# Gated mix of two 32-head attentions: one order of steps for a head, and one PSUM tile of seven banks

## The chip, the cores and the metric

The kernel runs on one core of one Trainium2 chip. The metric is the device time of one execution in microseconds (us): 2744.99 us, the median of three runs that lie between 2744.64 and 2745.0 us. The profile is of one more execution of the same program; its own span is 2743.5 us.

## The reference, cut to what matters

```python
def ref(x, wqkv, wo):                      # B=1, S=2048, D=512, H=32 heads of 16
    qkv = (x @ wqkv).reshape(B, S, 3, H, Dh).transpose(2, 0, 3, 1, 4)
    q, k, v = qkv[0], qkv[1], qkv[2]
    scores = einsum("bhqd,bhkd->bhqk", q, k) * (Dh ** -0.5)
    p = softmax(scores, axis=-1)
    o = einsum("bhqk,bhkd->bhqd", p, v)
    return o.transpose(0, 2, 1, 3).reshape(B, S, D) @ wo

g = sigmoid((x * gate_w).sum(-1, keepdims=True))
return g * ref(x, A_wqkv, A_wo) + (1 - g) * ref(x, B_wqkv, B_wo)
```

Two attentions over the same 2048 tokens give 64 heads in all, each with a 2048 x 2048 matrix of scores.

## The kernel before

**Prologue.** Queries, keys and values of both sides are projected by TensorE (`qk_tile`, `project_v`), each result as twelve accumulating matmuls into one PSUM bank of 128 x 512. ScalarE rounds a query or key tile (line 310), VectorE takes the rest of it (line 311), and both go to HBM; ScalarE copies a value tile out (line 346). There are 64 tiles of queries and keys and 32 of values. Between the value tiles, six at a time, the first 96 chunks of maxima are made.

**A head** is 16 rounds of 128 keys. Three kinds of work run over it, for three different heads or rounds at once:

- *Maxima, for a head two ahead.* The softmax needs each query's largest score. A chunk is one matmul of 128 queries by 512 keys (`scores_bank`, line 148) and a VectorE reduction of it (`max_plain`, line 153). In every second row block two chunks are made as a difference: ScalarE takes a Relu of one (`max_rise`, line 160), and VectorE adds it to the other while it reduces (`max_pair`, line 165). A head has 48 plain chunks, 8 rises and 8 pairs.
- *Scores and exponentials, for the present head.* A matmul of 128 keys by 512 queries (`score`, line 210), whose contraction also subtracts the maximum, and the exponential of it by ScalarE into the tile `p` (line 212); four of these fill a round, 64 a head.
- *Products with the values, two rounds behind* (`attend`, line 689). They accumulate in a PSUM bank of their own, `acc`. A quarter of a round is four small matmuls side by side; several quarters run as a burst. At a head's end ScalarE copies `acc` out (line 710).

Matmuls of the first two kinds contract over 48 or 50 rows, in the upper or the lower half of the array by turns (`rows`), so that two of them run side by side.

**What sets the order.** There is no scheduler: `tc.manual_schedule()` keeps the order in which the program is written, engine by engine, and the framework adds the waits on semaphores. The order comes from strings, four rounds at a time: `e` is a score with its exponential, `m` a plain maximum, `D` a rise, `A` a pair, and a digit a burst of so many quarters. `FULL` is used inside a head, `EDGE` where a head begins and ends, `LATE` once no maxima are left (the last 22 rounds). A head has 20 bursts: 16 of three quarters and 4 of four.

**PSUM.** Its eight banks are `acc`, three tiles of a pool `ps_m` and four of a pool `ps_st`. Each tile is one bank, handed out in rotation: maxima take from `ps_m`, scores and rises from `ps_st`. A matmul into a tile waits for the reader of that slot's tile before.

```python
    ps_m = ctx.enter_context(tc.tile_pool(name="ps_m", bufs=3, space=PSUM))
    ps_st = ctx.enter_context(tc.tile_pool(name="ps_st", bufs=4, space=PSUM))
    ps_acc = ctx.enter_context(tc.tile_pool(name="ps_acc", bufs=1, space=PSUM))
    acc = ps_acc.tile([P, 512], F32, name="acc")
```

The output projections (`project_out`, `project_part`, line 558) come in between, at bursts, when a side's heads are done, and once more at the end; each takes a bank from `result_bank`. Their 52 tiles are 16 of twelve matmuls, 15 of nine and 21 of three.

Of the kernel before, what the change touches and what calls it, by code (L numbers as in the profile page):

```python
# [32 lines left out]
P = 128  # L33
# [11 lines left out]
LEAD = 6  # L45
SCALE = DH ** -0.5
HALVES = (0, 64)
SC = 3 * DH


@with_exitstack
def gated_mha(ctx: ExitStack, tc: tile.TileContext, xT, x, wqkv_a, wo_a, wqkv_b, wo_b, gate_w, out):
# [29 lines left out]
    warm = ps_m.tile([P, 512], F32, name="ps_m")  # L82
    for i in range(14):
        pe.matmul(warm, ident, ident.unsqueeze(1).to_broadcast([P, 4, P]), start=True, stop=True)  # L84
    q_st, k_st, x_st = [], [], []
# [40 lines left out]
    mxp, rises = {}, {}  # L126
    turn = [0]

    def rows():
        turn[0] ^= 1  # L130
        return HALVES[1 - turn[0]]
# [6 lines left out]
    def scores_bank(m, c, early=False):  # L138
        h, t = divmod(m, NT)
        st = c == "rise" or early and c % 2  # L140
        ps = (ps_st if st else ps_m).tile([P, 512], F32, name="ps_st" if st else "ps_m")
        b = rows()
        q = q_st[h % 3]
        if c == "rise":
            k = x_st[h % 2][b:b + SC]
        else:
            k = k_st[h % 3][b:b + SC, c * 512:(c + 1) * 512]
        pe.matmul(ps, q[b:b + SC, t * P:(t + 1) * P], k, start=True, stop=True)  # L148
        return ps, mxp[h][:, t]
# [40 lines left out]
    ring = []  # L190

    def result_bank():
        if ring:
            ring[0] = (ring[0] + 1) % 7
        if not ring or ring[0] % 2:
            return ps_m.tile([P, 512], F32, name="ps_m")
        return ps_st.tile([P, 512], F32, name="ps_st")

    def score(r, c):
# [4 lines left out]
        kk, cc = (4 * (kt % 4) + c, kt // 4) if h == NH - 1 else (kt, c)  # L204
        b = rows()
        if r < 2 and c % 2:
            ps = ps_m.tile([P, 512], F32, name="ps_m")
        else:
            ps = result_bank() if ring else ps_st.tile([P, 512], F32, name="ps_st")
        pe.matmul(ps, k[b:b + SC + 2, kk * P:(kk + 1) * P], q[b:b + SC + 2, cc * 512:(cc + 1) * 512],  # L210
                  start=True, stop=True)
        act.activation(pt[r][:, c * 512:(c + 1) * 512], ps, AF.Exp, scale=SCALE)  # L212


    vpool = ctx.enter_context(tc.tile_pool(name="vpool", bufs=2))
# [10 lines left out]
    with tc.tile_pool(name="xs", bufs=1) as xs, tc.tile_pool(name="pro", bufs=2) as pro:  # L226
# [57 lines left out]
        def qk_tile(i, cc):  # L284
            s, g, isk = blocks[i]
            w = wblocks[s, isk * DM + g * P]
            ps = ps_st.tile([P, 512], F32, name="ps_st")
            steps = [(k, p) for p in PARTS for k in range(KC)]
            for n, (k, (a, b)) in enumerate(steps):
                pe.matmul(ps, w[a][:, k], (xh, xl)[b][cc][:, k], start=n == 0, stop=n == 3 * KC - 1)  # L290
            return ps

        def first_tiles():
            banks = [ps_st.tile([P, 512], F32, name="ps_st") for i in range(2)]
# [41 lines left out]
        def project_v(s, t):  # L336
            hi, lo = wblocks[s, 2 * DM]
            c, o = divmod(t * P, 512)
            ps = ps_st.tile([P, 512], F32, name="ps_st")
            n = 0  # L340
            for a, b in ((xh[c], hi), (xl[c], hi), (xh[c], lo)):
                for k in range(KC):
                    pe.matmul(ps, a[:, k, o:o + P], b[:, k], start=n == 0, stop=n == 3 * KC - 1)  # L343
                    n += 1
            v = ps.rearrange("p (h d) -> p h d", h=H)
            act.copy(v_st[t % 2][:, :, 0:16], v)  # L346
            nc.sync.dma_start(vd[s][t * P:(t + 1) * P, :], v_st[t % 2].rearrange("p h d -> p (h d)"))
# [373 lines left out]
            done[0] += qb - qa  # L721
            n -= qb - qa

    FULL = "mme3emmeem4meeemAe", "3emmeeem3meeemA3DeD"
    EDGE = "eemm4mDmemDe3emeemAe", "3emmeeem3emem3eAe"
    LATE = "ee4eeee4ee"
    projects, row_ops = [], []

    def due(first):
        for r in (first, first + 1):  # L730
            for fn, a in later.pop(r, ()):
                if fn is project_out:
                    projects.append(a)
                else:
                    fn(*a)
# [4 lines left out]
    to_rise = iter(range(first + 4, ROUNDS, 2))  # L740

    load_stacks(2)
    r = 2
    while r < ROUNDS:
        m = r + NT + LEAD
        if m >= ROUNDS and not ring:
            ring.append(6)
            turn[0] = 0
        order = (EDGE if r % NT == 2 and r > 2 else FULL)[0] + (EDGE if r % NT == 14 else FULL)[1]
        if m >= ROUNDS:  # L750
            order = LATE
        n = order.count("e") // 4
        due(r)
        if r % NT == 2 and r // NT + 2 < NH:
            if r // NT:
                load_stacks(r // NT + 2)
            new_maxima(r // NT + 2)
        scored = bursts = 0
        for step in order:
            if step == "e":  # L760
                if scored == 8:
                    due(r + 2)
                score(r + scored // 4, scored % 4)
                scored += 1
            elif step == "m":
                max_plain(*next(plain))
            elif step == "D":
                for k in to_rise:
                    max_rise(k)
                    break  # L770
            elif step == "A":
                max_pair(next(pairs))
            else:
# [11 lines left out]
        if m < ROUNDS and (m + 4) % NT == 0:  # L785
            row_ops += [(max_split, m // NT), (max_rows, m // NT)]
        r += n
    attend_next(4)
    for fn, a in mid.pop((ROUNDS - 2, 2)):
        fn(*a)  # L790
# [28 lines left out]
```

## Time and profile before

| | |
|---|---|
| median of three runs | 2744.99 us (2744.64 to 2745.0) |
| span of the profiled execution | 2743.5 us |
| instructions | 64283 |
| PE (TensorE matmul) busy | 2733.8 us, 100% |
| DVE (VectorE) busy | 2411.5 us, 88% |
| ACT (ScalarE) busy | 2410.8 us, 88% |
| POOL (GpSimd) busy | 262.2 us, 10% |
| DMA, mean | 84 GB/s |
| first products with the values | 289.1 us |

A busy PE is not a PE at its peak: matmuls overlap, and the end that the trace gives one is modelled. So the intervals between the starts of instructions are read here, not the shares. PEld is the load of a matmul's weights; it carries the wait for the bank, and the matmul follows it at once.

### The profile page before, as it was taken

To read this page: it belongs to the slowest core of one execution; us is meant where nothing else is said; L and a number is where in the kernel's file an instruction comes from. 1 tells how busy PE (TensorE), PEld (TensorE's weight loads), DVE (VectorE), ACT (ScalarE), POOL (GpSimd) and SP (SyncE) were. 2 spreads that over 40 slices of the span, in tenths; PEclk is the share of its full clock that TensorE was granted. 3 is DMA by queue.
4 is the path that set the end of the run, shared out by engine and by line. 5 is a ranking of instruction groups with operands and counts; after the bars stand their busy time and mean duration, and the time that the engine had idled before them with its cause. 6 is when DMAs were issued, how large, how long until landed. Compare 5 with 4: busy or idle time off the path is not lost.

```text
span 2743.5 us, 64283 instructions
## 1 busy us (share of the span) xinstructions
PE 2733.8 (100%) x25446; PEld 1418.7 (52%) x25446; DVE 2411.5 (88%) x4473; ACT 2410.8 (88%) x4794; POOL 262.2 (10%) x467
## 2 busy tenths in 40 slices
PE   9999999999999999999999999999999999999998
PEld 7787544444444444444444555544444444445543
DVE  5444899999999999999999978899999999998895
ACT  4222899999999999999999978899999999998787
POOL 2010112110000000000100232000000001002202
PEclk9999999999999999999999999999999999999999
DMA  8583434333333233333423534223333333344312
GB/s 286 181 262 153 93 74 81 62 70 62 74 67 60 52 60 67 62 64 62 85 52 54 123 78 92 48 49 62 78 62 63 59 66 65 62 87 83 80 36 95
DMA packets 95603, 231.25 MB, mean 84 GB/s; under 512 B 26182, under 2 KB 35878, under 8 KB 82758
## 3 DMA queue, kind: packets, MB, share of 16 engines
q1 hardware_dynamic: 91590, 216.65, 36.1%
q0 software_dynamic: 2560, 8.91, 1.1%
q8 instruction: 201, 3.29, 0.6%
q10 hardware_dynamic: 1152, 1.57, 0.2%
q14 instruction: 100, 0.82, 0.1%
HBM read 158.13 MB, written 68.94 MB: 83 GB/s over the span
## 4 chain that ended last, share of the span: by engine, by line
PE 99%; DVE 1%; DMA 0%; issue 0%; SPq 0%; DVEq 0%; POOL 0%; POOLq 0%
PE acc L689 38%; PE ps_st L210 24%; PE ps_m L148 19%; PE ps_st L290 6%; PE ps_st L148 5%; PE ps_st L343 3%; PE ps_m L558 3%; PE ps_st L558 0%; PE ps_m L84 0%; PE ps_st L299 0%; DVE o_acc L575 0%; DMA o_num<-od 0%; DVE mxp L153 0%; PE ps_m L210 0%; DVE rise L165 0%; DMA od<-ev 0%
## 5 line engine op out<-in xcount | busy, mean ns | idle before, releaser
L212 ACT ACTIVATE p<-ps_st 128x512 f32<-128x512 f32 x4050 | 2076.8, 629 | 95.3 <-PE ps_m L148 56.1
L153 DVE TENSOR_REDUCE mxp<-ps_m 128x1 f32<-128x512 f32 x3048 | 1934.8, 684 | 125.2 <-PE ps_st L148 46.0
L210 PE MATMUL ps_st<-q_st,k_st 50*128 50x512 f32 x4054 | 1269.5, 433 | 0.0
L148 PE MATMUL ps_m<-k_st,q_st 48*128 48x512 f32 x3548 | 1223.8, 439 | 0.3
L689 PE MATMUL acc<-p,vg 128*17 128x128 f32 (+3 forms) x15664 | 1129.8, 392 | 0.5 <-DVE ev L703 0.4
L210 PEld LDWEIGHTS ps_st<-q_st,k_st 50*128 50x128 f32 x4054 | 614.0, 184 | 436.4 <-ACT p L212 382.7
L148 PEld LDWEIGHTS ps_m<-k_st,q_st 48*128 48x128 f32 x3548 | 604.2, 184 | 268.7 <-DVE mxp L153 222.1
L689 PEld LDWEIGHTS acc<-p,vg 128*17 128x17 f32 x15664 | 323.1, 96 | 404.2 <-issue 330.7
L165 DVE CUSTOM_DVE_ANT_0 rise<-ps_m,rise 128x512 f32<-128x512 f32 x500 | 341.2, 682 | 16.6 <-PE ps_m L148 13.1
L160 ACT ACTIVATE rise<-ps_st 128x512 f32<-128x512 f32 x500 | 300.1, 601 | 16.6 <-PE ps_st L210 0.8
L148 PE MATMUL ps_st<-x_st,q_st 48*128 48x512 f32 x500 | 195.4, 451 | 0.0
L175 POOL CAST mparts<-mrow 128x16 fp32r<-128x16 f32 x64 | 12.7, 198 | 1875.9 <-DVE mrow L174 1875.9
L148 PEld LDWEIGHTS ps_st<-x_st,q_st 48*128 48x128 f32 x500 | 78.0, 184 | 119.5 <-ACT p L212 119.2
L310 ACT CAST part<-ps_st 128x512 fp32r<-128x512 f32 x64 | 37.0, 589 | 111.6 <-PE ps_st L290 95.6
L311 DVE TENSOR_TENSOR part<-ps_st,part 128x512 fp32r<-128x512 f32 x64 | 43.7, 690 | 93.7 <-ACT part L310 70.2
L346 ACT COPY v_st<-ps_st 128x512 f32<-128x512 f32 x32 | 18.8, 588 | 84.2 <-PE ps_st L343 82.5
L558 PE MATMUL ps_m<-wo,ot 128*128 128x512 f32 x348 | 83.0, 393 | 1.0
L558 PEld LDWEIGHTS ps_m<-wo,ot 128*128 128x128 f32 x348 | 64.4, 188 | 19.6 <-issue 4.6
L290 PE MATMUL ps_st<-xh,whi 128*128 128x512 f32 x224 | 59.9, 389 | 0.0
L290 PE MATMUL ps_st<-xh,wlo 128*128 128x512 f32 x224 | 59.9, 389 | 0.0
L290 PE MATMUL ps_st<-xl,whi 128*128 128x512 f32 x224 | 59.9, 389 | 0.0
L545 POOL TENSOR_TENSOR o_num<-o_num,rb 128x512 f32<-128x512 f32 x28 | 35.9, 1287 | 221.7 <-DMA rb<-rd 221.7
(120 smaller groups left out, 946.4 us busy)
## 6 DMA issues: line engine op xcount, KB each, us to landing
k_st<-kd SPq DMA_DIRECT2D x128, 256.0 KB
q_st<-qd SPq DMA_DIRECT2D x128, 256.0 KB
qd<-part SPq DMA_DIRECT2D x32, 512.0 KB
kd<-part SPq DMA_DIRECT2D x32, 512.0 KB
k_st<-kd SPq DMA_DIRECT2D x128, 128.0 KB
q_st<-qd SPq DMA_DIRECT2D x128, 128.0 KB
od<-ev SPq DMA_DIRECT2D x63, 256.0 KB
vd<-v_st SPq DMA_DIRECT2D x32, 272.0 KB
```

The source lines that it names most:

```text
L148: pe.matmul(ps, q[b:b + SC, t * P:(t + 1) * P], k, start=True, stop=True)
L153: dve.tensor_reduce(o[:, c:c + 1], ps, op=ALU.max, axis=AX.X)
L160: act.activation(rises[m], ps, AF.Relu)
L165: dve.tensor_tensor_reduce(out=rise, in0=ps, in1=rise, scale=1.0, scalar=LOWEST, op0=ALU.add, op1=ALU.max, accum_out=o[:, 0:1])
L210: pe.matmul(ps, k[b:b + SC + 2, kk * P:(kk + 1) * P], q[b:b + SC + 2, cc * 512:(cc + 1) * 512], start=True, stop=True)
L212: act.activation(pt[r][:, c * 512:(c + 1) * 512], ps, AF.Exp, scale=SCALE)
L290: pe.matmul(ps, w[a][:, k], (xh, xl)[b][cc][:, k], start=n == 0, stop=n == 3 * KC - 1)
L310: act.copy(pt[0][:, sl], ps)
L311: dve.tensor_tensor(pt[1][:, sl], ps, pt[0][:, sl].bitcast(F32), op=ALU.subtract)
L343: pe.matmul(ps, a[:, k, o:o + P], b[:, k], start=n == 0, stop=n == 3 * KC - 1)
L558: pe.matmul(ps, ot[a][:, slot, tt * P:(tt + 1) * P], wt[b][:, g], start=first and i == 0, stop=last and i == 2)
L689: pe.matmul(acc[32 * c:32 * c + 17, qa * P:qb * P], v[:, 4 * a + c if final else kt, j], p[:, c * 512 + qa * P:c * 512 + qb * P], start=fi ...
```

## The change

The three PSUM pools become one pool with two tiles: `acc`, and `ring`, one tile of seven banks of which every result takes a slice. `take` keeps the banks in the order of their last use and gives the oldest, or the one of a given rank. Up to the tenth round of the first head the prologue and the first rounds stay with three banks for the one use and four for the other. From there on, 62 times, a head's 16 rounds follow one string, `HEAD`, with the ranks of its banks in `RANKS`; a run of `q` is a burst of so many quarters, and `W` is two score matmuls into two banks and one exponential of 1024 over both. A head has 38 single exponentials and 13 wide ones, 48 plain maxima, 8 rises and 8 pairs as before, and 21 bursts (1 of one quarter, 2 of two, 13 of three, 5 of four). `r` marks the two small steps that close a head's maxima. `LATE` stays.

```diff
-    ps_m = ctx.enter_context(tc.tile_pool(name="ps_m", bufs=3, space=PSUM))
-    ps_st = ctx.enter_context(tc.tile_pool(name="ps_st", bufs=4, space=PSUM))
-    ps_acc = ctx.enter_context(tc.tile_pool(name="ps_acc", bufs=1, space=PSUM))
-    acc = ps_acc.tile([P, 512], F32, name="acc")
+    psum = ctx.enter_context(tc.tile_pool(name="psum", bufs=1, space=PSUM))
+    psb = psum.tile([P, NB, 512], F32, name="ring")
+    acc = psum.tile([P, 512], F32, name="acc")
+    age = list(range(NB))
+
+    def take(rank=0, among=range(NB)):
+        b = [b for b in age if b in among][rank]
+        age.remove(b)
+        age.append(b)
+        return b
+
+    def m_bank():
+        return psb[:, take(0, range(3))]
+
+    def st_bank():
+        return psb[:, take(0, range(3, NB))]
...
+    def chosen():
+        return psb[:, take(ranks.pop(0))] if ranks else None
...
-        ps = (ps_st if st else ps_m).tile([P, 512], F32, name="ps_st" if st else "ps_m")
+        ps = chosen() or (st_bank if st else m_bank)()
...
+        if n == 2:
+            b0, b1 = take(ranks.pop(0)), take(ranks.pop(0))
+            if b1 < b0:
+                chunks.reverse()
+            wide = [psb[:, b0], psb[:, b1]]
+            ps = psb[:, min(b0, b1):max(b0, b1) + 1:abs(b1 - b0)]
...
+        for i, c in enumerate(chunks):
+            kk, cc = (4 * (kt % 4) + c, kt // 4) if h == NH - 1 else (kt, c)
+            b = rows()
+            pe.matmul(wide[i] if n == 2 else ps, k[b:b + SC + 2, kk * P:(kk + 1) * P],
+                      q[b:b + SC + 2, cc * 512:(cc + 1) * 512], start=True, stop=True)
+        c = min(chunks)
+        p = pt[r][:, c * 512:(c + n) * 512]
+        act.activation(p.rearrange("p (n x) -> p n x", n=2) if n == 2 else p, ps, AF.Exp, scale=SCALE)
...
-    FULL = "mme3emmeem4meeemAe", "3emmeeem3meeemA3DeD"
-    EDGE = "eemm4mDmemDe3emeemAe", "3emmeeem3emem3eAe"
+    FULL = "mmeqqqemmeemqqqqmeeemAe", "qqqemmeeemqqqmeeemAqqqDeD"
+    HEAD = ('mqqqemmeemeqqmDemqmemreDqqqmeAmWqqqWAmeerqqqmDememqqqqemmWemqqqemWmmeqqqmeWDmqqq'
...
+    for h in range(1, NH - 1):
+        ranks.extend(int(x) for x in RANKS)
+        run(HEAD, h)
+        assert not ranks
```

What stands on TensorE in the middle of a head before, with the semaphores that a row waits for (Activation is ScalarE's count, DVE VectorE's; L210 is a score, L148 a maximum, L689 a product with the values):

```order
L689 MATMUL acc<-p,vg 17x256 x4
L210 MATMUL ps_st<-q_st_160,k_st_161 128x512 [waits Activation_49]
L148 MATMUL ps_m<-k_st_2348,q_st_2347 128x512 [waits DVE_49] x2
L210 MATMUL ps_st<-q_st_160,k_st_161 128x512 [waits Activation_49] x3
L148 MATMUL ps_m<-k_st_2348,q_st_2347 128x512 [waits DVE_49]
L689 MATMUL acc<-p,vg 17x256 x4
L689 MATMUL acc<-p,vg 17x128 x4
L148 MATMUL ps_m<-k_st_2348,q_st_2347 128x512 [waits DVE_49]
L210 MATMUL ps_st<-q_st_160,k_st_161 128x512 [waits Activation_49] x3
L148 MATMUL ps_m<-k_st_2348,q_st_2347 128x512 [waits DVE_49] x2
```

A score waits for ScalarE and a maximum for VectorE, whatever stands ahead of it. And the same place in the changed program (L233 is a score, L167 a maximum, L714 a product):

```order
L167 MATMUL ring<-k_st_160,q_st_159 128x512 [waits Activation_49]
L233 MATMUL ring<-q_st_2139,k_st_2140 128x512 [waits DVE_49]
L167 MATMUL ring<-k_st_160,q_st_159 128x512 [waits Activation_49]
L167 MATMUL ring<-k_st_160,q_st_159 128x512 [waits DVE_49]
L233 MATMUL ring<-q_st_2139,k_st_2140 128x512 [waits DVE_49]
L233 MATMUL ring<-q_st_2139,k_st_2140 128x512
L714 MATMUL acc<-p,vg 17x384 x4
L233 MATMUL ring<-q_st_2139,k_st_2140 128x512 [waits Activation_49]
L233 MATMUL ring<-q_st_2139,k_st_2140 128x512
L167 MATMUL ring<-k_st_160,q_st_159 128x512 [waits Activation_49]
L167 MATMUL ring<-k_st_160,q_st_159 128x512 [waits DVE_49]
L233 MATMUL ring<-q_st_2139,k_st_2140 128x512 [waits DVE_49]
```

Here the engine that a matmul waits for is the one that reads the result of the `ring` matmul ahead of it: ScalarE behind a score, VectorE behind a maximum; only the second matmul of a `W` (the rows without a wait) has none. The counts in the built program say the same. At one place a score goes to bank 0, and its exponential brings ScalarE's count to 1931; the next matmul, a maximum into bank 4, waits for 1931. Its reduction brings VectorE's count to 1969; the next, a maximum into bank 5, waits for 1969. Before, a score waited for the exponential four scores back.

The prologue, where six maxima (L148, now L167) stand between two value tiles (L343, now L368), before:

```order
L343 MATMUL ps_st<-wvlo,xh_180 128x512 x4
L148 MATMUL ps_m<-k_st_161,q_st_160 128x512
L148 MATMUL ps_st<-k_st_161,q_st_160 128x512 [waits DVE_49]
L148 MATMUL ps_m<-k_st_161,q_st_160 128x512
L148 MATMUL ps_st<-k_st_161,q_st_160 128x512 [waits DVE_49]
L148 MATMUL ps_m<-k_st_161,q_st_160 128x512
```

and now:

```order
L368 MATMUL ring<-wvlo,xh_174 128x512 x4
L167 MATMUL ring<-k_st_155,q_st_154 128x512 [waits Activation_49]
L167 MATMUL ring<-k_st_155,q_st_154 128x512 [waits DVE_49] x5
L368 MATMUL ring<-wvhi,xh_174 128x512 [waits DVE_49]
L368 MATMUL ring<-wvhi,xh_174 128x512 x3
```

Each of the six now waits, the first for the copy of the value tile ahead of it, the others for the maximum ahead of them, and the next value tile for the last of the six.

More of the change, by code (lines that the diff above doesn't have):

```diff
@@ L48 @@
 SC = 3 * DH
+NB = 7
 @with_exitstack
@@ L192, in result_bank, with score @@
     def result_bank():
[L193 to L199, printed above, removed]
+        return psb[:, take()] if ring else m_bank()
+    def score(r, c, n=1):
         h, kt = divmod(r, NT)
@@ L293, in first_tiles @@
         def first_tiles():
-            banks = [ps_st.tile([P, 512], F32, name="ps_st") for i in range(2)]
+            banks = [st_bank() for i in range(2)]
             for k in range(KC):
@@ L338, in project_v @@
             c, o = divmod(t * P, 512)
-            ps = ps_st.tile([P, 512], F32, name="ps_st")
+            ps = st_bank()
             n = 0
@@ L742, in gated_mha, with next_chunk, products, run @@
     load_stacks(2)
[L743 to L764, printed above, removed]
+    at_chunk = [2 * NQ]
+    def next_chunk(n=1):
+        r, c = divmod(at_chunk[0], NQ)
+        at_chunk[0] += n
+        if c == 0 and r % 2 == 0:
+            due(r)
+            if r % NT == 2 and r // NT + 2 < NH:
+                if r // NT:
+                    load_stacks(r // NT + 2)
+                new_maxima(r // NT + 2)
+        return r, c
+    def products(n):
+        for a in projects:
+            project_out(*a)
+        projects.clear()
+        turn[0] = 0
+        attend_next(n)
+        if row_ops:
+            fn, *a = row_ops.pop(0)
+            fn(*a)
+    def run(order, h=None):
+        steps = [fn for fn in (max_split, max_rows)]
+        i = 0
+        while i < len(order):
+            step = order[i]
+            n = 1
+            if step == "q":
+                n = len(order[i:]) - len(order[i:].lstrip("q"))
+                products(n)
+            elif step == "r":
+                steps.pop(0)(h)
+            elif step in "eW":
+                w = 2 if step == "W" else 1
+                score(*next_chunk(w), w)
             elif step == "m":
@@ L772, in gated_mha @@
                 max_pair(next(pairs))
+            i += n
+    cycle = FULL[0] + FULL[1]
+    run(cycle)
+    run(cycle[:-3] + "DeD".replace("D", "", 2))
+    for h in range(1, NH - 1):
+        ranks.extend(int(x) for x in RANKS)
+        run(HEAD, h)
+        assert not ranks
+    row_ops += [(max_split, NH - 1), (max_rows, NH - 1)]
+    r = at_chunk[0] // NQ
+    assert r + NT + LEAD == ROUNDS and done[0] == 4 * (r - 2)
+    ring.append(6)
+    turn[0] = 0
+    while r < ROUNDS:
+        due(r)
+        scored = bursts = 0
+        for step in LATE:
+            if step == "e":
+                if scored == 8:
+                    due(r + 2)
+                score(r + scored // 4, scored % 4)
+                scored += 1
             else:
```

25 lines of the change are left out of this document (12 added, 13 removed).

## The prediction

> **What bounds the kernel now.** I read the page first, then the waits, then the stretch of heads without output projections, then single instructions.
>
> ```profile
> span 2743.5 us, 64283 instructions
> PE 2733.8 (100%) x25446; PEld 1418.7 (52%) x25446; DVE 2411.5 (88%) x4473; ACT 2410.8 (88%) x4794; POOL 262.2 (10%) x467
> L212 ACT ACTIVATE p<-ps_st 128x512 f32<-128x512 f32 x4050 | 2076.8, 629 | 95.3 <-PE ps_m L148 56.1
> L153 DVE TENSOR_REDUCE mxp<-ps_m 128x1 f32<-128x512 f32 x3048 | 1934.8, 684 | 125.2 <-PE ps_st L148 46.0
> ```
>
> Three engines are nearly full. The per-head copy of `acc` is a clock: its starts in a quiet stretch give the time of a head.
>
> ```profile
> L710 ACT COPY ev<-acc x8: 587/592/594, 1028.6 to 1287.8; 128x512 f32<-128x512 f32 x8
> 1114.16 7.67 ACT L212 ACTIVATE p<-ps_st 128x512 f32<-128x512 f32 x15
> PEld ps_st L210 <- ACT p L212: 382.7, 879, 0.9
> PEld ps_m L148 <- DVE mxp L153: 222.1, 488, 0.9
> ```
>
> Seven heads in 259.2 us are 37.03 us each. ScalarE has 73 instructions in a head (64 exponentials, 8 rises, the copy), and fifteen in a row start (7.67 - 0.60) / 14 = 0.505 us apart: 73 of them are 36.9 us. So a head goes at ScalarE's pace, with VectorE and TensorE close behind, and this works only because the engines overlap: several banks are full at a time, and while ScalarE and VectorE each empty one, TensorE fills the next. TensorE's waits for a reader, the last two rows, are short ones (0.9 us at the longest).
>
> **What the change does to that.** By its words it lets all results share seven banks and spares 13 starts of an exponential. But the order above shows another thing: in the changed program each matmul into `ring` waits for the reader of the one ahead of it, whatever bank that used, because the seven banks are now one tile. Then matmul, reader, matmul, reader form one chain, with one bank in use, and the seven are worth nothing. The price of the chain is a round trip, and its four parts have rows:
>
> ```profile
> 1112.17 0.50 PE L148 MATMUL ps_st<-x_st,q_st 48*128 48x512 f32 x1
> 1112.71 0.60 ACT L160 ACTIVATE rise<-ps_st 128x512 f32<-128x512 f32 x1
> ...
> 1076.67 0.60 ACT L160 ACTIVATE rise<-ps_st 128x512 f32<-128x512 f32 x1
> 1077.32 0.18 PEld L210 LDWEIGHTS ps_st<-q_st,k_st 50*128 50x128 f32 x1 [0.19 <-ACT rise L160]
> ...
> 256.36 0.50 PE L148 MATMUL ps_m<-k_st,q_st 48*128 48x512 f32 x1
> 256.89 0.69 DVE L153 TENSOR_REDUCE mxp<-ps_m 128x1 f32<-128x512 f32 x1 [2.64 <-PE ps_st L148]
> ...
> 1104.37 0.68 DVE L153 TENSOR_REDUCE mxp<-ps_m 128x1 f32<-128x512 f32 x1
> 1105.10 0.18 PEld L148 LDWEIGHTS ps_m<-k_st,q_st 48*128 48x128 f32 x1 [0.22 <-DVE mxp L153]
> ```
>
> A matmul into an idle array takes 0.50; ScalarE starts 0.54 after its start, works 0.60, and 0.05 after its end (1077.27 to 1077.32) the released load begins. *A ScalarE step is 0.54 + 0.60 + 0.05 = 1.19 us.* VectorE starts 0.53 after, works 0.69, and 0.05 later (1105.05 to 1105.10) comes the load: *a VectorE step is 1.27 us.* A pair's instruction is of the same size as a reduction (682 against 684 ns in the page), so it counts as one.
>
> *A wide step.* No exponential of 1024 is in the trace. Its two matmuls have no wait between them and go side by side; the length of the reader I take from a ScalarE cast that comes in both widths.
>
> ```profile
> L277 ACT CAST xh<-raw 128x512 fp32r<-128x512 f32 x8 | 4.9, 618 | 1.2 <-DMA raw<-in_xT 1.0
> L277 ACT CAST xh<-vg 128x1024 fp32r<-128x1024 f32 x4 | 4.1, 1054 | 0.0
> ...
> 1108.46 0.50 PE L210 MATMUL ps_st<-q_st,k_st 50*128 50x512 f32 x1
> 1108.46 0.49 PE L148 MATMUL ps_m<-k_st,q_st 48*128 48x512 f32 x1
> ```
>
> 512 more elements cost 1.054 - 0.618 = 0.44, so 0.54 + 0.60 + 0.44 + 0.05 = 1.63. Bounds: 1.2 if the width were free, 2.4 if it were two steps; the cast is the nearest row, and the bounds move a head by 13 x 0.4 to 0.8 us.
>
> *The bursts* do not touch `ring`, so they run while the reader of the last matmul works.
>
> ```profile
> 1103.28 0.39 PE L148 MATMUL ps_m<-k_st,q_st 48*128 48x512 f32 x1
> 1103.60 1.05 PE L689 MATMUL acc<-p,vg 128*17 128x512 f32 x8
> 1104.58 0.18 PEld L148 LDWEIGHTS ps_m<-k_st,q_st 48*128 48x128 f32 x1 [0.85 <-DVE mxp L153]
> ...
> 1111.40 0.84 PE L689 MATMUL acc<-p,vg 128*17 128x384 f32 x8
> 1112.17 0.18 PEld L148 LDWEIGHTS ps_st<-x_st,q_st 48*128 48x128 f32 x1 [0.64 <-ACT p L212]
> ```
>
> A burst begins 0.32 after the last matmul (0.43 behind one of 0.50 instead of 0.39) and holds TensorE 0.77 for three quarters, 0.98 for four. Three quarters end at 1.20, under the step that hides them. Four end at 1.41: 0.14 beyond a VectorE step, 0.22 beyond a ScalarE step. Of the five, three stand behind a maximum, one behind a single score and one behind a `W` (hidden): 0.64 us a head. If the reader did not cover them, 21 bursts would cost 16 us a head.
>
> *A head:* 38 + 8 ScalarE steps (46 x 1.19 = 54.7), 48 + 8 VectorE steps (56 x 1.27 = 71.1), 13 wide steps (21.2), bursts 0.6: 147.7 us against 37.03. The order of `HEAD`, its ranks, and the starts it spares on ScalarE (13 x about 0.07) change nothing in this sum, since no engine is full any more. 62 heads: 9,157 us.
>
> *The rest of the program* uses `ring` too.
>
> ```profile
> L310 ACT CAST part<-ps_st 128x512 fp32r<-128x512 f32 x64 | 37.0, 589 | 111.6 <-PE ps_st L290 95.6 <-DMA qd<-part 12.3 <-DVE rise_k L320 2.0
> L311 DVE TENSOR_TENSOR part<-ps_st,part 128x512 fp32r<-128x512 f32 x64 | 43.7, 690 | 93.7 <-ACT part L310 70.2
> L346 ACT COPY v_st<-ps_st 128x512 f32<-128x512 f32 x32 | 18.8, 588 | 84.2 <-PE ps_st L343 82.5
> 61.76 0.59 ACT L310 CAST part<-ps_st 128x512 fp32r<-128x512 f32 x1 [2.13 <-PE ps_st L290]
> 64.48 0.59 ACT L310 CAST part<-ps_st 128x512 fp32r<-128x512 f32 x1 [1.61 <-PE ps_st L290]
> 262.93 0.50 PE L148 MATMUL ps_m<-k_st,q_st 48*128 48x512 f32 x1
> L689 PE MATMUL acc<-raw,vg x32: 272/386/498, 289.1 to 293.1; 128*17 128x384 f32 x16, 128*17 128x128 f32 x16
> ```
>
> The prologue lasts to 289.1 us. A query or key tile takes 2.72 there (61.76 to 64.48), 0.227 a matmul. Chained it is 11 x 0.227 + 0.39 for the last, then 0.04, ScalarE 0.59, 0.03, VectorE 0.69, 0.05: 4.28, 1.56 more, x 64 = 100. A value tile: 2.88 + 0.04 + 0.59 + 0.05 = 3.56, 0.84 more, x 32 = 27. Two value tiles with six maxima take 6.57 (256.36 to 262.93), so a maximum 0.19; chained 1.27, x 96 = 104 more. Ten first scores and rises: 10 more. Prologue 530. The first eight rounds (28 VectorE and 36 ScalarE steps) are 78, the last 22 rounds 88 x 1.19 + 22 bursts x 0.2 = 109. The 52 output tiles, at 0.23 for each matmul but the last and 0.50 + 0.05 + 0.69 + 0.05 for that one and its reader, are 16 x 3.8 + 15 x 3.1 + 21 x 1.75 = 144; the sums at the end and the last stores 17.
>
> Sum: 530 + 78 + 9,157 + 109 + 144 + 17 = 10,035 us against the span of 2743.5; the median lies 1.5 above it. I predict **10,040 us**. Were the matmul 0.39, as behind another one, a head would fall by 115 x 0.11 and the time to 9,250; were each step 0.05 longer, as the mean exponential (629 ns) is against the 0.60 used, it would be 10,400. Own range 9,500 to 10,450.
>
> **Rivals.** *First, the wait is by bank after all* (the slice, not the tile, decides on the chip, and the waits in the order are met early). It decides from the point where a matmul starts before the reader ahead of it has ended. Then the change does what it says: 13 x (0.505 - 0.44) = 0.9 us of ScalarE a head, 56 in all, is the most it can gain, 2,690; nothing if TensorE, with 21 bursts for 20, takes over: 2,745. I would say 2,715: not slower. Against it stand the counts in the built program; for it, only that nothing in the data asks for such a wait. [...]
>
> *Second, the array's clock.* In the chain TensorE streams little.
>
> ```profile
> 2737.50:2740.90 3.40, 0.00 (x0) 0.00 (x0) 1.32 (x3) 0.00 (x0) 0.94 (x1) 1.00 0.99 380
> 2741.00:2743.50 2.50, 0.00 (x0) 0.00 (x0) 0.00 (x0) 0.00 (x0) 0.00 (x0) 0.50 0.27 105
> 1.38 4.87 PE L84 MATMUL ps_m<-ident 128*128 128x512 bf16 x11 [1.38 <-POOL ident masks.py:199]
> 1.38 5.30 PE L84 MATMUL ps_m<-ident 128*128 128x512 bf16 x12 [1.38 <-POOL ident masks.py:199]
> ```
>
> After the last matmul the granted clock stays 1.00 for 3.4 us without work and is 0.50 from then on; at the start, before it has risen, matmuls come 0.43 apart instead of 0.23. If a half-empty array is enough for 0.50, a step grows by 0.20 (streaming alone) to 0.50 (all of the matmul), 115 x that = 23 to 58 a head, and longer bursts show 3 to 14 beyond the step: 174 to 219 a head, 11,750 to 14,600 with the rest. The row nearest is the streaming one: 12,000. Against it: the pauses in the chain are under 1 us, and the one pause that the trace shows to lower the clock is 3.4. [...]
>
> **How the numbers follow.** A chain at full clock 0.65, a chain at the half clock for most of the time 0.25, waits by bank 0.05, a chain that I have mis-sized beyond its range 0.05. The range reaches from the first case's lower end to the nearer half of the second: 9,500 to 12,400. A difference of 0.2% is about what a measurement of this kernel can tell from none: faster 0.03, same 0.02 (both from the waits by bank), slower 0.95.
>
> **What would show it.** In the changed profile a head should last about 148 us between copies of `acc`; ScalarE and VectorE should be near a quarter busy; nearly all idle time of PEld should be put down to the last reader, ScalarE's or VectorE's, and that of the readers to PE; a maximum should start 1.2 to 1.3 us after the one ahead of it, and wide exponentials be near 1.04 us. A granted clock under 1.00 in the heads makes the second rival right; a head of 36 to 37 us the first.

## The result, and the profile after

The changed kernel takes 13,060.64 us (median; 13,054.63 to 13,062.47) against 2744.99 us before. The ratio is 4.757, with a 95% interval of 4.751 to 4.764. The prediction was 10,040 us in a range of 9,500 to 12,400. The chain that it describes is there, but each turn of it is longer than it said.

The page of the changed kernel:

```profile
span 13058.9 us, 62481 instructions
PE 8126.6 (62%) x24950; PEld 2822.1 (22%) x24950; DVE 2644.1 (20%) x4473; ACT 2724.6 (21%) x3988; POOL 259.1 (2%) x467
PEclk8755555555555555555555555555555555555555
L237 ACT ACTIVATE p<-ring 128x512 f32<-128x512 f32 (+1 forms) x3282 | 2302.9, 702 | 8700.4 <-PE ring L233 8700.4
L172 DVE TENSOR_REDUCE mxp<-ring 128x1 f32<-128x512 f32 x3096 | 2141.4, 692 | 8408.0 <-PE ring L167 8408.0
```

ScalarE and VectorE do the work they did before and wait for TensorE the rest of the time. The view of waits of the same kernel shows that TensorE for its part waits for them (columns: total us, times, longest):

```profile
PEld ring L167 <- ACT p L237: 2815.0, 2183, 1.7
PEld ring L233 <- DVE mxp L172: 2051.7, 1614, 1.3
```

A maximum (L167) waits for an exponential and a score (L233) for a reduction, neither of which reads its bank: that is the chain. The third row of the page is what the forecast had not taken as likeliest. The granted clock is 0.85 in the first 300 us and 0.50 to 0.52 on average from the heads on.

Where a head's time goes is seen in its timeline (start, length, engine, instruction):

```profile
5006.09 0.80 PE L233 MATMUL ring<-q_st,k_st 50*128 50x512 f32 x2 [0.78 <-DVE mxp L172]
5006.81 1.48 PE L714 MATMUL acc<-p,vg 128*17 128x384 f32 x8
5006.97 1.02 ACT L237 ACTIVATE p<-ring 128x1024 f32<-128x1024 f32 x1 [4.09 <-PE ring L233]
5008.22 0.29 PEld L233 LDWEIGHTS ring<-q_st,k_st 50*128 50x128 f32 x2 [1.26 <-ACT p L237]
...
5010.14 0.28 PEld L167 LDWEIGHTS ring<-k_st,q_st 48*128 48x128 f32 x1 [1.62 <-ACT p L237]
...
5011.72 0.79 PE L167 MATMUL ring<-k_st,q_st 48*128 48x512 f32 x1 [0.79 <-DVE mxp L184]
5012.55 0.69 DVE L172 TENSOR_REDUCE mxp<-ring 128x1 f32<-128x512 f32 x1 [0.89 <-PE ring L167]
5013.29 0.28 PEld L233 LDWEIGHTS ring<-q_st,k_st 50*128 50x128 f32 x1 [1.29 <-DVE mxp L172]
...
5014.83 0.28 PEld L233 LDWEIGHTS ring<-q_st,k_st 50*128 50x128 f32 x1 [1.25 <-ACT p L237]
5016.97 0.28 PEld L167 LDWEIGHTS ring<-k_st,q_st 48*128 48x128 f32 x1 [1.26 <-ACT p L237]
...
5020.02 0.79 PE L233 MATMUL ring<-q_st,k_st 50*128 50x512 f32 x1 [0.69 <-ACT rise L179]
5020.85 0.60 ACT L237 ACTIVATE p<-ring 128x512 f32<-128x512 f32 x1 [0.88 <-PE ring L233]
5021.50 0.28 PEld L167 LDWEIGHTS ring<-k_st,q_st 48*128 48x128 f32 x1 [1.19 <-ACT p L237]
```

Readers last as forecast: 0.60 and 0.69, and 1.02 for a wide exponential. The matmul lasts 0.79 instead of 0.50. So a ScalarE step is 21.50 - 20.02 = 1.48 (forecast 1.19), a VectorE step 13.29 - 11.72 = 1.57 (1.27), a wide step 10.14 - 8.22 = 1.92 (1.63): each 0.29 or 0.30 longer. And bursts stand out of their cover: three quarters hold TensorE 8.22 - 6.81 = 1.41 (0.77 before), and the step of 14.83 to 16.97 that holds such a burst takes 2.14 instead of 1.48.

The copies of `acc` give a head's time, and three exponentials divide the program: the first behind the prologue, the first under `HEAD`, and the first of the last 22 rounds:

```profile
L735 ACT COPY ev<-acc x62: 585/585/585, 803.9 to 12737.7; 128x512 f32<-128x512 f32 x62
...
613.97 0.60 ACT L237 ACTIVATE p<-ring 128x512 f32<-128x512 f32 x1 [4.03 <-PE ring L233]
...
714.35 0.60 ACT L237 ACTIVATE p<-ring 128x512 f32<-128x512 f32 x1 [3.04 <-PE ring L233]
...
12839.61 0.60 ACT L237 ACTIVATE p<-ring 128x512 f32<-128x512 f32 x1 [2.46 <-PE ring L233]
```

A head takes (12737.7 - 803.9) / 61 = 195.6 us. By steps it is 46 x 1.48 + 56 x 1.57 + 13 x 1.92 = 181.0; the 14.6 left are bursts and output tiles. Of the forecast's 144 us for the output tiles, the first 31 (107 us) fall into the heads and 21 (37 us) to the end:

| | forecast | measured | more |
|---|---|---|---|
| prologue | 530 | 614 | 84 |
| first eight rounds | 78 | 100 | 22 |
| 62 heads, with 31 output tiles | 9,157 + 107 | 12,125 | 2,861 |
| last 22 rounds, 21 tiles, end | 109 + 37 + 17 | 219 | 56 |
| sum | 10,035 | 13,059 | 3,024 |

The heads hold 95% of what was not forecast. The prologue's part, at a clock of 0.85, was not taken apart.

### The profile page after: what moved, and what is told of

The parts are those of the page before. It is cut to its first block, busy times and chain, and to the rows that moved or that the text cites. A ratio compares the mean times of both kernels' runs of the same rounds, so it can differ in the third digit from the quotient of the medians.

```text
span 13058.9 us, 62481 instructions
## 1 busy us (share of the span) xinstructions
PE 8126.6 (62%) x24950; PEld 2822.1 (22%) x24950; DVE 2644.1 (20%) x4473; ACT 2724.6 (21%) x3988; POOL 259.1 (2%) x467
## 3 DMA queue, kind: packets, MB, share of 16 engines
q10 hardware_dynamic: 1152, 1.57, 0.0%
## 4 chain that ended last, share of the span: by engine, by line
PE 62%; DVE 17%; ACT 17%; issue 4%; DMA 0%; ACTq 0%; SPq 0%; DVEq 0%
PE ring L167 25%; PE ring L233 20%; PE acc L714 14%; ACT p L237 14%; DVE mxp L172 14%; DVE rise L184 2%; ACT rise L179 2%; PE ring L315 1%; PE ring L583 1%; PE ring L368 1%; DVE part L336 0%; ACT part L335 0%; DVE o_acc L600 0%; ACT v_st L371 0%; DVE mxp L184 0%
## 5 line engine op out<-in xcount | busy, mean ns | idle before, releaser
L167 PE MATMUL ring<-k_st,q_st 48*128 48x512 f32 x3596 | 2824.9, 786 | 2485.3 <-ACT p L237 1437.6
L237 ACT ACTIVATE p<-ring 128x512 f32<-128x512 f32 (+1 forms) x3282 | 2302.9, 702 | 8700.4 <-PE ring L233 8700.4
L172 DVE TENSOR_REDUCE mxp<-ring 128x1 f32<-128x512 f32 x3096 | 2141.4, 692 | 8408.0 <-PE ring L167 8408.0
L233 PE MATMUL ring<-q_st,k_st 50*128 50x512 f32 x4096 | 2599.5, 789 | 1918.9 <-DVE mxp L172 1078.3
L714 PE MATMUL acc<-p,vg 128*17 128x128 f32 (+3 forms) x15168 | 2008.0, 655 | 0.0
L167 PEld LDWEIGHTS ring<-k_st,q_st 48*128 48x128 f32 x3596 | 1015.6, 282 | 4466.7 <-ACT p L237 2561.0
L233 PEld LDWEIGHTS ring<-q_st,k_st 50*128 50x128 f32 x4096 | 936.3, 284 | 4020.2 <-DVE mxp L172 2051.7
L184 DVE CUSTOM_DVE_ANT_0 rise<-ring,rise 128x512 f32<-128x512 f32 x500 | 345.9, 692 | 1453.3 <-PE ring L167 1453.3
L167 PE MATMUL ring<-x_st,q_st 48*128 48x512 f32 x500 | 394.8, 790 | 357.4 <-DVE mxp L172 243.2
L714 PEld LDWEIGHTS acc<-p,vg 128*17 128x17 f32 x15168 | 396.3, 122 | 761.9 <-issue 741.0
L179 ACT ACTIVATE rise<-ring 128x512 f32<-128x512 f32 x500 | 298.5, 597 | 1027.5 <-PE ring L167 1027.5
L167 PEld LDWEIGHTS ring<-x_st,q_st 48*128 48x128 f32 x500 | 141.7, 283 | 657.8 <-DVE mxp L172 400.4
L368 PE MATMUL ring<-wvhi,xh 128*128 128x512 f32 x128 | 54.0, 560 | 25.3 <-DVE mxp L172 12.5
```

What stands on the lines that cost most here:

```text
L172: dve.tensor_reduce(o[:, c:c + 1], ps, op=ALU.max, axis=AX.X)
L179: act.activation(rises[m], ps, AF.Relu)
L184: dve.tensor_tensor_reduce(out=rise, in0=ps, in1=rise, scale=1.0, scalar=LOWEST, op0=ALU.add, op1=ALU.max, accum_out=o[:, 0:1])
L233: pe.matmul(wide[i] if n == 2 else ps, k[b:b + SC + 2, kk * P:(kk + 1) * P], q[b:b + SC + 2, cc * 512:(cc + 1) * 512], start=True, stop=True)
L237: act.activation(p.rearrange("p (n x) -> p n x", n=2) if n == 2 else p, ps, AF.Exp, scale=SCALE)
L714: pe.matmul(acc[32 * c:32 * c + 17, qa * P:qb * P], v[:, 4 * a + c if final else kt, j], p[:, c * 512 + qa * P:c * 512 + qb * P], start=fi ...
```

## The experiments

### Seven tiles instead of one

The new order and its table of ranks, with seven tiles of one bank each. Two tiles have no common slice, so a wide exponential becomes two of 512.

```diff
-    psb = psum.tile([P, NB, 512], F32, name="ring")
+    bank = [psum.tile([P, 512], F32, name=f"ring{i}") for i in range(NB)]
...
-        act.activation(p.rearrange("p (n x) -> p n x", n=2) if n == 2 else p, ps, AF.Exp, scale=SCALE)
+        for i, c in enumerate(chunks):
+            act.activation(pt[r][:, c * 512:(c + 1) * 512], wide[i] if n == 2 else ps, AF.Exp, scale=SCALE)
```

> The changed order with its ranks of banks, but the seven banks are seven tiles of one bank, and a W is two matmuls with two exponentials of 512 (64 a head again). Theory (the one tile makes the chain, the chain lets the array's clock fall): the waits go by bank, heads last 36.3 to 37.5 us between copies of acc, the clock is 1.00, and the time is 2,700 to 2,780 us. Rival (the new order itself, or the ranks, stall the engines): heads stay far above 40 us and the time above 3,000. From the rows of before: 21 bursts for 20 cost TensorE 0.1 us a head against its floor, and shared banks may give back part of the 0.9 us that TensorE waits in a head.

Measured: 2756.05 us (2755.34 to 2760.02), 1.004 times the kernel before (1.0026 to 1.0055). Its span and clock, and its groups of exponentials and of reductions:

```profile
core 0: 2758.0 us, clock 0.998
L235 ACT ACTIVATE p<-ring 128x512 f32<-128x512 f32 x4088 | 2128.6, 630 | 117.8 <-PE ring L232 83.7 <-PE ring L167 0.7
L172 DVE TENSOR_REDUCE mxp<-ring 128x1 f32<-128x512 f32 x3096 | 1951.9, 683 | 111.0 <-PE ring L167 83.7 <-PE ring L232 7.5
```

The idle time ahead of the reductions has gone from 8408.0 to 111.0 us. The order and its ranks are not the loss.

### One tile in the kernel before

The old order, old rotation and 64 single exponentials; only the seven banks of `ps_m` and `ps_st` are slices of one tile.

```diff
-    ps_m = ctx.enter_context(tc.tile_pool(name="ps_m", bufs=3, space=PSUM))
-    ps_st = ctx.enter_context(tc.tile_pool(name="ps_st", bufs=4, space=PSUM))
+    psb = psum.tile([P, 7, 512], F32, name="ring")
...
```

> The kernel before with its order, its three and four banks in rotation and no wide exponential; only, the seven banks are slices of one tile. Theory: the tile alone makes the chain. At the half clock a ScalarE step is 1.48 us and a VectorE step 1.57 by the changed kernel's trace, so a head has 72 x 1.48 + 56 x 1.57 = 194.5 us and about 13 us of bursts, some 208 against 195.6 in the changed kernel, and the time is about 13,800 us. Rival (the order or the ranks carry the loss): under 3,500 us.

Measured, in a single run: 13,986 us at a clock of 0.520, near the 13,800 expected. The layout of the seven banks alone costs a factor of five; the order, the rotation and the exponentials are those of before. A head:

```profile
L719 ACT COPY ev<-acc x62: 585/585/585, 811.7 to 13654.9; 128x512 f32<-128x512 f32 x62
```

It is 210.5 us, 14.9 more than the changed kernel's. Most of that is the price of 26 ScalarE steps for 13 wide ones: 13 x (2 x 1.48 - 1.92) = 13.5. So inside the chain the wide exponentials do pay.

### Two tiles

Maxima in a tile of three banks, scores and rises in one of four; wide exponentials stay.

```diff
-    psb = psum.tile([P, NB, 512], F32, name="ring")
+    tm = psum.tile([P, 3, 512], F32, name="ring_m")
+    ts = psum.tile([P, 4, 512], F32, name="ring_s")
...
```

> The changed kernel with two tiles instead of one: three banks for maxima, four for scores and rises (the oldest of its own each time, wide exponentials kept). Theory (a tile is what a matmul waits for): two chains that can run beside each other, one of 56 VectorE steps and one of 46 ScalarE steps and 13 wide ones a head. At full clock they are 71 and 76 us long, at half clock 88 and 93; TensorE's own order makes each wait for the other at times, so a head should lie between 75 and 130 us, the time between 5,100 and 8,500. Rival (something other than the tile serializes): 13,000 us as before.

Measured, in a single run: 8,288 us, clock 0.533, near the upper end of what was expected. The waits, and the copies of `acc`:

```profile
PEld ring_s L237 <- ACT p L241: 1744.4, 1462, 1.8
PEld ring_m L171 <- DVE mxp L176: 1384.0, 1094, 1.5
...
L739 ACT COPY ev<-acc x62: 586/586/586, 661.2 to 8063.6; 128x512 f32<-128x512 f32 x62
```

Now a score waits for ScalarE and a maximum for VectorE. Two chains side by side, each at its own pace, would need 46 x 1.48 + 13 x 1.92 = 93 us a head at half clock; measured are 121.4. The timeline suggests what lies between. Bursts stand in the way of both chains: at one place a burst begins at 4013.49, VectorE is done at 4014.29, and the next maximum starts only at 4015.33, when the burst is over, together with the next score. And the program fixes TensorE's order, so a matmul that waits for one chain holds up the other chain's behind it: the waits put 1084.0 us of VectorE's down to a score's matmul and 983.3 us of ScalarE's to a maximum's. How much each of the two costs was not measured.

### One unread matmul in each gap

What lowers the clock? The changed kernel, with a ring of six banks, and behind each score and maximum one matmul whose result nobody reads.

```diff
+    def keep_busy():
+        for _ in range(1):
+            pe.matmul(idle, ident, ident.unsqueeze(1).to_broadcast([P, 4, P]), start=True, stop=True)
...
```

> The changed kernel with one bank less in the ring, and behind each score and each maximum (once behind the two of a W) a matmul of 512 bf16 columns into that bank, which nobody reads. It runs while the reader works, so it lengthens no step at full clock (0.23 us in a step of 1.19). Theory (a half-empty array is what lowers the clock): the granted clock rises well above 0.52, towards 1.00; at 1.00 a head is 148 us and the time 10,000 to 10,100. If the clock stays at 0.50, the added matmul takes 0.43 beside the reader and the time stays at 13,000 to 13,300. Rival (the step is long for another reason than the clock): the clock rises and the steps stay 1.48 and 1.57.

Measured, in a single run: 13,741 us, clock 0.524. The theory missed, and so did the 13,000 to 13,300 that stood for an unchanged clock. The windows view from 1000 to 11,000 us (PE busy first, PEclk after POOL), and some of the timeline:

```profile
1000.00:11000.00 10000.00, 8864.25 (x23661) 2518.32 (x23653) 1913.38 (x3252) 2009.04 (x2916) 135.09 (x289) 0.51 0.07 13
...
5001.72 0.61 PE L146 MATMUL idle<-ident 128*128 128x512 bf16 x1
5002.47 0.28 PEld L239 LDWEIGHTS ring<-q_st,k_st 50*128 50x128 f32 x1 [0.65 <-ACT p L244]
...
5003.20 0.61 PE L146 MATMUL idle<-ident 128*128 128x512 bf16 x1
5003.74 1.91 PE L721 MATMUL acc<-p,vg 128*17 128x512 f32 x8
```

By the record TensorE is now busy for 89% of the time, and the clock is still 0.51. A ScalarE step is unchanged, 5002.47 - 5001.00 = 1.47, since the unread matmul (0.61) fits beside the reader; a burst begins 0.54 later (3.20 to 3.74) because it queues behind it. For 21 bursts in each of 62 heads that is 703 us, and the run is 681 us slower than the changed kernel.

### Two unread matmuls in each gap

> The changed kernel with a ring of six banks, and behind each score and maximum matmul two matmuls of 128x512 in bf16 whose results nobody reads (all else is computed as before). [...] In the chain at 0.50 a step of 1.48 us holds one score matmul (about 0.43 of streaming) and with one filler 0.85, 58%: no rise, as that run showed. [...] Expected: clock 0.8 to 1.0, and a time of 10,050 to 11,500 us. Rival (the array's clock doesn't go by its own work in these kernels): clock at 0.52, and 14,000 to 14,600 us, since every burst queues behind one more filler at half clock.

The edit is `range(2)` in the lines above. Measured, in a single run: 11,418 us at a clock of 0.90, that is 1,643 us less with 14,772 matmuls more. Windows over the same 10,000 us, and over a stretch at full clock with the one behind it; then two steps in that stretch:

```profile
1000.00:11000.00 10000.00, 8759.95 (x35489) 2482.72 (x35489) 2327.16 (x3948) 2436.05 (x3533) 188.26 (x370) 0.90 0.08 16
...
5012.00:5073.40 61.40, 52.50 (x237) 15.28 (x229) 15.38 (x28) 15.88 (x23) 0.47 (x3) 1.00 0.00 1
5073.40:5090.40 17.00, 17.00 (x47) 4.14 (x50) 2.88 (x5) 2.99 (x5) 0.00 (x0) 0.50 0.02 4
...
5047.75 0.50 PE L239 MATMUL ring<-q_st,k_st 50*128 50x512 f32 x1
5048.18 0.60 PE L146 MATMUL idle<-ident 128*128 128x512 bf16 x2
5048.94 0.18 PEld L172 LDWEIGHTS ring<-k_st,q_st 48*128 48x128 f32 x1 [0.64 <-ACT p L244]
5050.22 0.18 PEld L239 LDWEIGHTS ring<-q_st,k_st 50*128 50x128 f32 x1 [0.74 <-DVE mxp L178]
```

Clock and time lie where the run was expected. The second unread matmul is the one difference from the run before, and with it the mean clock went from 0.524 to 0.90. At full clock a ScalarE step is 48.94 - 47.75 = 1.19 and a VectorE step 50.22 - 48.94 = 1.28, the forecast's 1.19 and 1.27, against 1.48 and 1.57 at 0.50: the price of the clock is one apart from the chain's.

### Unread matmuls where no burst follows

> As the run with two unread matmuls behind each score and maximum matmul (ring of six banks, 11,418 us at a clock of 0.90), but these are left out where a burst of value products follows, so that no burst queues behind them. Theory (the chain as the prediction priced it, and the clock by the array's own work): the bursts are hidden again, a step at full clock is 1.19 and 1.28 us, and the sum of the prediction, 10,035 us, is met at a clock near 1.00; with the clock at 0.50 for a tenth of the time, up to 10,700. Rival (other costs beside the clock were left out of the sum): above 10,900 with a clock over 0.9.

Measured, in a single run: 12,863 us, clock 0.626. Both expectations missed. Without the unread matmuls at the 21 bursts of a head the mean clock was 0.626 instead of 0.90. But the run has stretches at full clock, and in them the bursts follow the chain's matmuls directly, as in the prediction. One such stretch, and two steps in it, the first with a burst of four quarters, the second with one of three:

```profile
4271.40:4332.80 61.40, 50.87 (x229) 15.14 (x229) 16.61 (x26) 16.70 (x24) 0.00 (x0) 1.00 0.19 33
...
4277.33 0.49 PE L175 MATMUL ring<-k_st,q_st 48*128 48x512 f32 x1
4277.75 1.05 PE L725 MATMUL acc<-p,vg 128*17 128x512 f32 x8
4278.73 0.18 PEld L175 LDWEIGHTS ring<-k_st,q_st 48*128 48x128 f32 x1 [0.85 <-DVE mxp L181]
...
4306.44 0.50 PE L175 MATMUL ring<-k_st,q_st 48*128 48x512 f32 x1 [0.58 <-ACT p L248]
4306.87 0.84 PE L725 MATMUL acc<-p,vg 128*17 128x384 f32 x8
4307.72 0.18 PEld L243 LDWEIGHTS ring<-q_st,k_st 50*128 50x128 f32 x1 [0.72 <-DVE mxp L181]
```

The step with four quarters takes 78.73 - 77.33 = 1.40 (forecast 1.41), and the one with three takes 7.72 - 6.44 = 1.28, a VectorE step and no more: the burst is hidden. In the same stretch a wide step takes 82.81 - 81.20 = 1.61 (forecast 1.63), and three quarters behind a score make a step of 86.62 - 85.37 = 1.25 where 1.20 was forecast. So each part of the forecast's head was seen at full clock with nearly its forecast price; a whole head of the chain at full clock (147.7 us) was measured in no run.

### Order by bank, one tile and the wide exponentials kept

The changed kernel in all but one thing: TensorE's, ScalarE's and VectorE's instructions on `ring` are ordered against those that use the same bank, and not against others. A wide exponential is ordered against every bank from its first to its last.

```diff
+        for name, engine, other in self.seen:
+            if engine is not self.engine and not other & banks:
+                self.tc.declare_no_dep(inst, group=name, keep=[i for g, i in keep if g == name], reason="other banks")
+        for b in banks:
+            for engine, last in self.last.setdefault(b, {}).items():
+                if engine != self.name:
+                    self.tc.add_manual_dep(inst, last, mybir.DependencyInfo(
+                        mybir.DependencyClass.Sync, mybir.DependencyReason.DATA), reason="the same bank")
...
```

> The changed kernel, with its tile of seven banks, its order and its 13 wide exponentials, but an instruction on the ring is ordered only against those of other engines on its own bank (a wide exponential, whose two banks may lie apart, against all banks from the one to the other). Theory (the loss is the order by tile and nothing else): the time of seven single tiles, 2,756, less what the wide exponentials save on ScalarE if that still sets the pace, up to 0.7 us a head, 45 us: 2,700 to 2,770, clock 0.99 to 1.00. Rival (the wide exponentials make chains of their own, since up to five banks between their two wait with them): 13 a head, 0.5 to 1.2 us each, 400 to 1,000 us: 3,150 to 3,750.

Measured: 4028.68 us (4013.41 to 4038.77), ratio 1.467 (1.464 to 1.469), clock 0.797. This is on the rival's side, and more than the rival named. The clock fell too; what share of the loss is the clock's was not measured. The waits:

```profile
DVE mxp L64 <- PE ring L64: 1083.4, 838, 3.8
PEld ring L64 <- ACT p L64: 999.5, 934, 2.8
ACT p L64 <- PE ring L64: 928.0, 845, 14.6
```

(All operations have line 64 here, that of the helper.) TensorE again waits for exponentials, 1.07 us at a time. Of the 806 wide exponentials 464 use banks that lie apart. The next three runs take those away, and the loss goes with them. The exponentials themselves are no slower for it (1.028 us on average here, 1.029 with neighbours only), so it is the order that costs. Whether the banks between the two have to be included was not tested.

### Wide exponentials on neighbouring banks

Three variants of the kernel by bank. In the first, each wide exponential takes the pair of neighbours that has lain longest. In the second, the table's banks stay; only the 342 pairs that happen to be neighbours are wide, and the others are two of 512. In the third, the second bank is a neighbour of the first where one is among the two oldest: 544 wide.

```diff
+            near = abs(b1 - b0) == 1
...
+        if n == 2 and not near:
+            for c, ps in zip(chunks, wide):
+                act.activation(pt[r][:, c * 512:(c + 1) * 512], ps, AF.Exp, scale=SCALE)
+            return
```

> As the one by bank, but each wide exponential takes the two neighbouring banks that have lain longest, so that it is ordered against two banks alone. Theory (order by tile and nothing else): 2,700 to 2,770, within 0.5% of the one by bank. Rival (wide exponentials bind the banks between): 2,700 to 2,770 here, where the one by bank is above 3,150. Rival (the table of ranks no longer fits, and matmuls wait for banks read late): 2,780 to 2,900.

> The kernel ordered by bank, with the change's own table of ranks; a wide exponential where its two banks are neighbours (342 of the 806), two of 512 where they are not. Theory (a wide exponential costs more than it saves, since its two banks come free late and together): between seven single tiles (2,756) and neighbouring pairs (2,803), by its share 2,770 to 2,785. Rival (the choice of neighbours cost the 47 us, and a wide exponential saves ScalarE time): 2,735 to 2,755.

> As the kernel with wide exponentials where the table's two banks are neighbours (342 of 806 wide, 2,751 us), but the second bank is a neighbour of the first wherever one is among the two oldest, which makes 544 wide. Theory (a wide exponential saves a little where its banks come free in time, and only forced choices cost): 2,742 to 2,750, at best level with the kernel before. Rival (each departure from the table costs, as with neighbours always, 2,803): 2,752 to 2,790.

| wide exponentials, of 806 | us | ratio to before (95%) |
|---|---|---|
| none (seven tiles) | 2756.05 | 1.0040 (1.0026 to 1.0055) |
| 342, the table's own neighbours | 2750.65 | 1.0019 (1.0010 to 1.0028) |
| 544 | 2747.87 | 1.0008 (0.9999 to 1.0017) |
| 806, oldest neighbours | 2803.02 | 1.0211 (1.0198 to 1.0224) |

The clock is 0.998 or more in all four. By the medians a wide exponential saves about (2756.05 - 2750.65) / 342 = 0.016 us where its banks fit, and the next 202 about as much. But the intervals of the first three rows overlap, each with the next, and no run ordered by bank does without wide exponentials altogether, so a saving is likely but not shown. Choosing neighbours against the table costs 2%, which is clear of that noise. So my theory for the second run, that a wide exponential costs more than it saves, was wrong, and its rival's range holds the time; the third went as the theory formed from that said, and the first as its second rival. The third is level with the kernel before, within its interval; no variant is faster.

### The order alone, the shared banks alone

First the new order with banks divided as before, three for maxima and four for scores and rises, without wide exponentials. Then the old order with all seven banks in one pool, taken in turn.

```diff
-        ps = chosen() or (st_bank if st else m_bank)()
+        ps = (st_bank if st else m_bank)()
...
```

```diff
-    ps_m = ctx.enter_context(tc.tile_pool(name="ps_m", bufs=3, space=PSUM))
-    ps_st = ctx.enter_context(tc.tile_pool(name="ps_st", bufs=4, space=PSUM))
+    ps_m = ps_st = ctx.enter_context(tc.tile_pool(name="ring", bufs=7, space=PSUM))
...
```

> The changed order of steps with single tiles of one bank, three for maxima and four for scores and rises as before, the oldest first; each wide exponential is two of 512. Theory (the shared banks serve the new order, which alone is worse): 2,770 to 2,850. Rival (the order alone is what cost 0.4%, banks don't matter): 2,750 to 2,762.

> The kernel before with its own order, its seven banks in one ring of single tiles that maxima and scores take in turn. Theory (more banks for whoever comes next are slack, and ScalarE's pace rules): 2,735 to 2,760. Rival (taking in turn lets a slow reader hold up the other engine's matmul): 2,770 to 2,950.

Measured: the order alone 2809.31 us, ratio 1.0232 (1.0218 to 1.0246); the banks alone 2868.33 us, 1.0448 (1.0433 to 1.0462). A wait of the second kernel that comes to 0.7 us in all in the kernel before (L209 is a score):

```profile
PEld ring L209 <- DVE mxp L152: 232.2, 426, 0.6
```

Scores there wait for VectorE's readers, whichever bank the turn brings. So the theory held for the order, and the rival for the banks. Each part alone costs 2.3 and 4.5%; together, with the table of ranks, they cost 0.4%. The order and the ranks fit each other, and the division into three and four fits the old order. No run had the old order with the oldest of the seven banks, or the new order with shared banks and no ranks.

## Why the prediction was right in kind and wrong in size

- **A chain by tile: right.** Every matmul waits for the reader ahead of it. Seven tiles remove the loss, and one tile in the kernel before brings it.
- **The reader's parts of a step: right.** 0.60, 0.69 and 1.02 (forecast 1.04), with the same gaps of 0.03 to 0.05.
- **The matmul's part: the step that failed.** The working put "a matmul into an idle array takes 0.50" into all 115 steps. Measured 0.79: 115 x 0.29 = 33 us a head. At full clock the steps are as forecast (1.19, 1.28 and 1.61), which the last two runs with unread matmuls show, so the sum's method held and its clock did not.
- **"The bursts are hidden": failed with it.** Three quarters take 1.41 at half clock, and a step that holds them 2.14 instead of 1.48; at full clock they were hidden, or nearly so. Bursts and the output tiles together left 14.6 us a head where 0.6 and 1.7 had stood.
- **The second rival came true, at a chance of 0.25.** Its range, 11,750 to 14,600, holds the time. Its own number, 12,000, was taken at the row for streaming alone (0.20 a step); the whole isolated matmul adds 0.29.
- **The argument against that rival was wrong.** It was that the chain's pauses are under 1 us and the one pause seen to lower the clock is 3.4 us. The end of the kernel before shows one pause of 3.4 us with a clock of 0.50 behind it; that a pause of that length is needed did not follow. In the changed kernel the clock fell at 609.35 us, and TensorE's pauses in the 3.41 us before were 0.72 us at the most.
- **The range.** It reached only to the nearer half of the second rival, at 12,400. With a chance of 0.25 on a case of 11,750 to 14,600, it left out the part in which the time then lay.
- **The first rival (waits by bank): refuted** for the kernel as written. Its price for the change done as meant was 2,690 to 2,745, with 2,715 as the likeliest. The nearest kernel measured, with 544 of the 806 exponentials wide, takes 2747.87 and is level with the kernel before: the upper end of that price, and no gain.

## What to carry to other kernels

Before putting several banks into one tile, count which reader each matmul waits for: in this kernel, slices of one tile were ordered as if they were one buffer, and seven buffers became one. When a chain leaves TensorE partly idle, price its matmuls at half clock as well: here they took 0.79 instead of 0.50, at a clock of 0.50 with TensorE busy for 62% and no wait of a matmul above 1.3 us. An order of steps and the rotation of its buffers belong together: here each of them alone cost more than both.

## What the runs showed of the hardware

The granted clock went to 0.50 in the changed kernel without any long pause: at 609.35 us it fell behind 3.41 us in which TensorE was busy for 1.96 and stood still for 0.72 at the most. The windows view over the longest stretch at 0.50 and over what ends it; then TensorE's costliest wait in that stretch, and its longest, which stands ahead of the output tile that ends it:

```profile
609.35:7337.02 6727.67, 4159.32 (x12784) 1359.66 (x12785) 1359.25 (x2312) 1433.83 (x2087) 104.21 (x231) 0.50 0.07 13
7333.61:7337.02 3.41, 3.41 (x9) 2.65 (x9) 0.00 (x0) 0.00 (x0) 0.00 (x0) 0.50 0.00 0
7337.02:7354.09 17.07, 11.82 (x50) 7.25 (x49) 4.32 (x8) 1.02 (x1) 6.83 (x9) 1.00 0.00 0
...
PE ring L167 <- ACT p L237: 858.4, 1073, 1.2
...
7332.32 5.16 PE L583 MATMUL ring<-wo,ot 128*128 128x512 f32 x12 [1.26 <-ACT p L237]
```

For 6,728 us the clock stays at 0.50, though no wait of a matmul there is longer than 1.3 us and TensorE is busy for 62%. It rises after 3.41 us without a gap (an output tile of twelve matmuls), holds for 17 us at 69% busy, and falls when the chain goes on. In the trace's list of the clock's changes every stretch but the last, which the end of the trace cuts, is a whole multiple of 3.41 us. Divided into such stretches, the changed kernel has 41 falls, each behind a stretch recorded as 57% busy or less, and 40 rises, each behind one of 82% or more. The recorded busy time does not tell when the clock changes: stretches of 46 and 52% (80.28 and 114.42 us) brought no fall, some 290 above 82% brought no rise, a mean of 89% went with a clock of 0.51 in the run with one unread matmul, and a matmul alone is recorded with 0.50 us at full clock where dense ones follow each other every 0.23. What decides was not shown.

In the run with two unread matmuls the clock swings: 1.00 for 61 us at 86% busy, then 0.50 for 17 us at 100%. In the changed kernel it swings in the prologue (0.85 over the first 300 us) but is 0.50 to 0.52 on average from the heads on.
